# Stores of the high parts of parked weights: issued from GpSimd, one operation later, in place of ScalarE

## The chip, the core and the metric

The kernel runs on one core of one Trainium2 chip. The metric is the device time of one execution in microseconds, from the first to the last instruction of the core.

## What is computed

Causal attention over 4 batches, 8 heads, 576 positions and 64 features (four heads with a local window of 32 positions, four with a stride of 32), and behind it two gated feed-forward blocks over 2304 tokens, with 512 features and 1536 hidden ones. Cut to what matters:

```
scores = q @ k.T / 8, masked; attn = softmax(scores); x = attn @ v      # x: 2304 x 512
xn = x / sqrt(mean(x*x) + 1e-6) * rms_g
x  = (silu(xn @ w1_gate) * (xn @ w1_val)) @ w1_out
out = (silu(x @ w2_gate) * (x @ w2_val)) @ w2_out
```

All tensors are float32. The kernel forms each float32 product with fp32r matmuls: it splits each operand into a high and a low part and sums three products, high x high, high x low and low x high.

## The kernel before, in words

**Tiling and stages.** Three stages overlap. Attention (the class Attention, in program order up to about 260 us of the trace) makes x in pieces. The first four chunks of the first block's hidden features run beside it and a little after it, in plain products of 128 x 512 tokens (`gate`, `down`). From then on a *block stage* runs over five passes of four chunks and three stretches of 768 tokens each (the loop over `work` at the end). There each pair of projections, gate and value, is done with seven products of quarter size in place of eight: sums and differences of quarters of the weights and of the tokens go in. A chunk's weights are therefore sums of quarters (`QUARTERS`), split into high and low.

**The weights' way.** A `combined_step(m, c, how)` prepares gate and value weights of chunk c. Its operations are: load the two raw blocks (`fetch`, SP's queue), decode them with ScalarE and VectorE (`scale`, lines 279 to 296), form four sums of quarters on GpSimd (`sum_`, line 385), and split the four groups into high and low. `first` (line 424) casts the high part on ScalarE, `second` (line 431) subtracts it on VectorE for the low part. With how = "park" the parts go to DRAM instead of staying in SBUF: both parts lie in the step's own raw and dh buffers, `first` sends the high part off ScalarE's queue, and `save` (line 438) sends the low part off SP's. A later `recall_step` loads both back (`w<-pk`), 512 KB or 256 KB at a time. The buffers raw (three) and dh (two) are reused by the next step once both stores have landed. There are sixteen steps with how = "park" (the words with p in `plan`): p14 to p17 first, twelve in the block stage.

**The order.** The operations of a step run in the order of this list, one at a time, between the matmuls of other work:

```
ops = [op(i, f) for i, f in ((0, first), (0, second), (1, first), (0, save), (1, second), (2, first), (1, save), (2, second),
                             (3, first), (2, save), (3, second), (3, save))]
```

`point()` is called every few matmuls; it advances attention's phases and, through `weights()`, starts operations at the rate `pace["op"]` (0.7 to 1.0 per point in the block stage). `behind(eng)` puts an instruction after the engine's last important one in program order; `paced` makes a GpSimd instruction wait for a given matmul. Within these rules the framework orders each engine's queue, and every engine runs its queue in order.

**GpSimd's other work** is the normalisation of attention's exponentials (`e`, line 700), sums of token quarters (lines 1169 and 1339), the weights' sums (line 385), and in the block stage the low halves of the next stretch's tokens:

```
with behind("act"):
    nc.scalar.copy(out=xh[:, kk], in_=src[:, kk])
paced(nc.gpsimd.tensor_tensor(out=xl[:, kk], in0=src[:, kk], in1=xh[:, kk].bitcast(F32), op=ALU.subtract), ("pe", None))
```

(lines 1357 and 1358.) GpSimd issues two transfers of its own, loads of k for the first batch (line 554).

**ScalarE's other work** near the change: attention's exponentials (line 683), copies out of PSUM (line 87: pT, qT, kT, x), the casts of tokens (line 981), and in the block stage the copies and activations of lines 1415 to 1439.

Of the kernel before, what the change touches and what calls it, by code (L numbers as in the profile page):

```python
# [8 lines left out]
F32 = mybir.dt.float32  # L9
# [16 lines left out]
def attn_ffn_ffn(ctx: ExitStack, tc: tile.TileContext, q, k, v, w1g, w1v, w1o, rms_g, w2g, w2v, w2o, out):  # L26
    nc = tc.nc
# [19 lines left out]
    dp = ctx.enter_context(tc.tile_pool(name="dp", bufs=1, space=DRAM))  # L47
# [92 lines left out]
    def paced(ins, by="act"):  # L140
        if by in last:
            tc.add_manual_dep(ins_of(ins), (last[by][2] if by == ("pe", None) else last[by]).name, mybir.DependencyInfo(mybir.DependencyClass.Sync, mybir.DependencyReason.DATA),
                              reason="pace")
# [10 lines left out]
    def send(out, in_):  # L154
        n = 4
        for w in out.shape:
            n *= w
        line[0] = max(line[0], clock[0]) + n / state['rate']
        nc.sync.dma_start(out=out, in_=in_)
# [61 lines left out]
    def take(key, kb):  # L221
        place = room[kb].pop(0)
        held.setdefault(key, []).append((kb, place))
        return place
# [5 lines left out]
    def home(place, w, name):  # L230
        pool, tag = place
        return pool.tile([128, 2, w], F32R, tag=tag, name=name)
# [6 lines left out]
    def back(bk, n):  # L239
        bk["back"].append((clock[0] + (6 if n else 0) + state["slack"], n))  # L240
# [7 lines left out]
    def spent(bk, n):  # L248
        bk["wback"].append(clock[0] + n)
        bk["wback"].sort()  # L250

    def spaces():
        bk = racks[0]
        while bk["back"] and bk["back"][0][0] <= clock[0]:
            bk["free"] += bk["back"].pop(0)[1]
        return bk["free"]
# [3 lines left out]
    def fetch(m, c, z, cell):  # L260
        bk = cell["bk"] = racks[0]
        bk["free"] -= 1
        w = WSRC[m][z].bitcast(U32)
        if z == 2:
            src = w[c * 128:(c + 1) * 128, :].rearrange("p (k f) -> p k f", k=KC)
        else:
            src = w[:, c * 256:(c + 1) * 256].rearrange("(k p) f -> p k f", p=128)
        r = bk["pool"].tile([128, KC, 256], U32, tag="raw", name="raw", bufs=bk["bufs"])
        send(out=r, in_=src)
        words = r.rearrange("p k f -> p (k f)").rearrange("p (n s) -> p n s", s=2)  # L270
        cell.update({"raw": r, "lw": words[:, :, 0], "hw": words[:, :, 1]})
# [84 lines left out]
    def combined_step(m, c, how):  # L356

        g, v = {}, {}
        at = []
        parts = []  # L360
        got = {}
        n4 = 2 if how == "split" else 3

        def ready():
            if spaces() < 2:
                return False
            return how == "park" or len(room[4]) >= n4 and len(room[2]) >= 7 - 2 * n4

        def load():
            if how != "park":  # L370
                at.extend([take((m, c, False), 4) for _ in range(n4)] + [take((m, c, False), 2) for _ in range(7 - 2 * n4)])
            fetch(m, c, 0, g)
            fetch(m, c, 1, v)

        def source(z):
            flat = g["raw"].rearrange("p k f -> p (k f)").bitcast(F32)
            t = flat.rearrange("p (a n) -> p a n", a=4)
            b11, b21 = g["h"][:, 0:256], g["h"][:, 256:512]
            b12, b22 = v["h"][:, 0:256], v["h"][:, 256:512]
            return flat, t, b22, {0: (b12, b11), 2: (b22, b12), 1: (b22, t[:, 0]), 3: (b21, t[:, 1])}[z]  # L380

        def sum_(z):
            def f():
                _, t, _, (a, b) = source(z)
                paced(nc.gpsimd.tensor_tensor(out=t[:, z], in0=a, in1=b, op=ALU.subtract))  # L385
            return f

        def sums():
            sum_(3)()
            flat, _, b22, _ = source(0)  # L390
            spaces = v["raw"].rearrange("p k f -> p (k f)").bitcast(F32)
            src = {0: g["h"], 1: flat[:, 0:512], 2: flat[:, 512:1024], 3: b22}
            his = {0: spaces[:, 0:512], 1: spaces[:, 512:1024], 2: spaces[:, 0:512], 3: v["h"][:, 0:256]}
            for i in (0, 3, 1, 2) if how != "park" else (0, 1, 3, 2):
                w = 256 * len(QUARTERS[i])
                if how == "park":
                    parts.append((QUARTERS[i], src[i], his[i].bitcast(F32R), src[i].bitcast(F32R), i))
                    continue
                if how == "split" and i == 1:
                    places = [(q_, src[i][:, 256 * j:256 * j + 256], at[n4 + 1 + j]) for j, q_ in enumerate(QUARTERS[i])]  # L400
                    places = [((q_,), a, p) for q_, a, p in places]
                else:
                    places = [(QUARTERS[i], src[i], at[n4] if i == 3 else at[min(i, n4 - 1)])]
                for qs, a, place in places:
                    t_ = home(place, 256 * len(qs), f"w{m}_{c}_{qs[0]}")
                    parts.append((qs, a, t_[:, 0], t_[:, 1], t_))

        stores = {}

        def op(i, f):  # L410
            def g_():
                f(*parts[i])
                if f is (save if how == "park" else second) and parts[i][0][0] in (1, 3):
                    spent((g if parts[i][0][0] == 1 else v)["bk"], 6 if how == "park" else 8)
                if i == len(parts) - 1 and f is (save if how == "park" else second):
                    back(g["bk"], 1)
                    if how == "park":
                        back(v["bk"], 1)
                    else:
                        wt[m, c, 0] = got  # L420
                        wdone.add((m, c, 0))
            return g_

        def first(qs, a, hi_, lo_, t_):
            with behind("act"):
                nc.scalar.copy(out=hi_, in_=a)
                if how == "park":
                    stores[t_] = d = dp.tile([128, 2, 256 * len(qs)], F32, name=f"pk{m}_{c}_{t_}")
                    nc.scalar.dma_start(out=d[:, 0], in_=hi_.bitcast(F32))

        def second(qs, a, hi_, lo_, t_):
            with behind("dve"):
                nc.vector.tensor_tensor(out=lo_, in0=a, in1=hi_.bitcast(F32), op=ALU.subtract)
            if how != "park":
                for j, q_ in enumerate(qs):
                    got[q_] = t_[:, :, 256 * j:256 * j + 256]

        def save(qs, a, hi_, lo_, t_):
            d = stores[t_]
            send(out=d[:, 1], in_=lo_.bitcast(F32))  # L440
            parked.setdefault((m, c), {})[t_] = d

        k = 5 if how == "split" else 4
        lag = 1 if how == "park" else 2
        if how == "park":
            ops = [op(i, f) for i, f in ((0, first), (0, second), (1, first), (0, save), (1, second), (2, first), (1, save), (2, second),
                                         (3, first), (2, save), (3, second), (3, save))]
            ops[2].late = 1
        else:
            ops = [op(i, f) for i in range(k) for f in (first, second)]  # L450
            ops[lag * 2].late = 1
        sv = scale(v, int(how != "park"))
        sv[0].late = 0.6
        return Step([load] + scale(g, 0) + sv + [sum_(0), sum_(2), sum_(1), sums] + ops, ready, PRIO_W)
# [26 lines left out]
    def behind(eng):  # L481

        return tc.issue_after(last[eng]) if eng in last else nullcontext()
# [1064 lines left out]
    for n, (m, cs, t0) in enumerate(work):  # L1548
# [88 lines left out]
        c = chunks[-1]  # L1637
# [47 lines left out]
```

## Time and profile before

| | |
|---|---|
| median of 3 runs | 1016.6 us (1012.5 to 1017.88) |
| the profiled execution's own time, and its span | 1012.5 us |
| TensorE busy | 967.9 us, 5987 matmuls |
| VectorE, ScalarE, GpSimd busy | 579.2, 576.7, 387.0 us |
| transfers on ScalarE's queue (q10) | 14.68 MB, 4.0% of the time of 16 DMA engines |
| transfers on SP's queue (q1) | 203.72 MB, 61.8% |
| transfers on GpSimd's queue (q0) | 0.28 MB, 0.1% |

The profile is of one execution. Busy time counts instructions that compute; the issue of a transfer is not counted on ScalarE and SP (rows marked ACTq and SPq in the timelines). In the rows, ACT is ScalarE, DVE VectorE, POOL GpSimd, PE TensorE, SP the engine that issues most transfers. `out<-in` are the program's names of tiles; pk is the store in DRAM, raw and dh the step's buffers, w a weight tile, xh and xl a token tile's high and low part. PEclk is the granted clock of TensorE as a share of full speed. An entry in brackets is idle time of the engine just before the instruction, and what ended it.

### The profile page before, as it was taken

Reading aid. Unit: us, or ns where it says so; the run is one execution under the profiler, and the core shown is the slowest. Engines: PE = TensorE matmul, PEld = TensorE weight load, DVE = VectorE, ACT = ScalarE, POOL = GpSimd, SP = SyncE. Lnnn points to the kernel's source line nnn. Section 1 sums busy time; section 2 is a strip of 40 time slices with the busy share of each in tenths; the row PEclk is TensorE's granted clock in tenths of the full one; section 3 lists DMA queues with packets and bytes.
Section 4 is the critical chain, followed back from the end, with each engine's and each line's share of the span. In section 5 each row is a group of like instructions: output and inputs, shape, how many; then the busy total and the mean of one; then the engine's idle time right before and its main releaser. Section 6 shows DMA issues by size and latency. Waiting matters only on the chain.

```text
span 1012.5 us, 17613 instructions
## 1 busy us (share of the span) xinstructions
PE 967.9 (96%) x5987; PEld 889.2 (88%) x5987; DVE 579.2 (57%) x1294; ACT 576.7 (57%) x1449; POOL 387.0 (38%) x417
## 2 busy tenths in 40 slices
PE   5789998799999999999999999999999999999998
PEld 4677876577989999998999999999999999999997
DVE  2886575777434665465655566554556655653333
ACT  5988586674344645464655555555646655563431
POOL 3221052352050546270716464663517243441500
PEclk9988999899999999999999999999999999999999
DMA  7775647955978374988667777637887397865211
GB/s 185 208 227 184 171 127 218 290 187 184 341 236 295 118 242 153 319 285 287 193 204 264 261 223 252 200 132 281 271 299 269 123 309 249 307 203 174 83 65 63
DMA packets 171602, 219.81 MB, mean 217 GB/s; under 512 B 47092, under 2 KB 125116, under 8 KB 171512
## 3 DMA queue, kind: packets, MB, share of 16 engines
q1 hardware_dynamic: 162104, 203.72, 61.8%
q10 hardware_dynamic: 9216, 14.68, 4.0%
q8 instruction: 47, 0.77, 0.3%
q14 instruction: 43, 0.35, 0.1%
q0 software_dynamic: 192, 0.28, 0.1%
HBM read 146.80 MB, written 71.83 MB: 216 GB/s over the span
## 4 chain that ended last, share of the span: by engine, by line
PE 70%; DMA 3%; ACT 2%; DVE 1%; issue 0%; SPq 0%; DVEq 0%; ACTq 0%
PE b_y L76 32%; PE b_a L76 17%; PE b_g L76 11%; PE b_v L76 10%; DMA pk<-raw 1%; DMA pk<-dh 1%; DMA raw<-in_moe_w_gate_dram 0%; DMA xq<-xst 0%; ACT xh L1357 0%; ACT dh L279 0%; ACT hh L1439 0%; ACT t L1415 0%; ACT raw L287 0%; DVE dh L296 0%; ACT t L1429 0%
## 5 line engine op out<-in xcount | busy, mean ns | idle before, releaser
L1358 POOL TENSOR_TENSOR xl<-xst,xh 128x384 fp32r<-128x384 f32 x196 | 212.2, 1105 | 177.4 <-PE b_y L76 78.0
L76 PE MATMUL b_y<-xh,w 128*128 128x384 f32 x784 | 211.4, 335 | 2.6 <-ACT t L1415 2.2
L76 PEld LDWEIGHTS b_y<-xh,w 128*128 128x128 f32 x784 | 142.9, 188 | 5.7 <-ACT t L1415 3.1
L76 PE MATMUL b_a<-xh,w 128*128 128x384 f32 (+2 forms) x512 | 141.0, 335 | 0.8 <-ACT t L1415 0.7
L76 PE MATMUL b_y<-xl,w 128*128 128x384 f32 x392 | 131.4, 335 | 0.0
L76 PE MATMUL b_g<-xh,w 128*128 128x384 f32 (+2 forms) x416 | 127.6, 348 | 2.2 <-ACT w L304 1.5
L76 PE MATMUL b_v<-xh,w 128*128 128x384 f32 (+2 forms) x352 | 108.1, 350 | 2.0 <-ACT t L1429 1.3
L76 PEld LDWEIGHTS b_a<-xh,w 128*128 128x128 f32 x512 | 93.2, 188 | 4.1 <-ACT t L1415 1.8
L1357 ACT CAST xh<-xst 128x384 fp32r<-128x384 f32 x196 | 91.5, 520 | 0.0
L385 POOL TENSOR_TENSOR raw<-dh 128x256 f32<-128x256 f32 x40 | 29.4, 754 | 150.9 <-DVE dh L296 56.3
L76 PE MATMUL b_a<-xl,w 128*128 128x384 f32 (+2 forms) x256 | 85.8, 335 | 0.0
L76 PEld LDWEIGHTS b_g<-xh,w 128*128 128x128 f32 x416 | 77.4, 191 | 7.9 <-ACT w L304 1.7
L76 PE MATMUL b_y<-hh,w 128*128 128x384 f32 (+2 forms) x304 | 80.7, 341 | 0.0
L76 PEld LDWEIGHTS b_y<-xl,w 128*128 128x128 f32 x392 | 73.6, 188 | 1.8
L700 POOL TENSOR_TENSOR e<-e,rc 128x384 f32<-128x384 f32 (+3 forms) x40 | 36.3, 915 | 98.4 <-DVE nb L674 23.4
L76 PEld LDWEIGHTS b_v<-xh,w 128*128 128x128 f32 x352 | 64.9, 190 | 7.9 <-ACT t L1429 1.7
L76 PE MATMUL b_g<-xl,w 128*128 128x384 f32 (+2 forms) x208 | 70.3, 338 | 0.0
L76 PE MATMUL b_y<-w,hh 128*128 128x512 f32 x216 | 67.1, 391 | 0.0
L683 ACT ACTIVATE e<-e,nb 128x96 f32<-128x96 f32 (+2 forms) x152 | 56.6, 376 | 13.6 <-DVE nb L674 9.6
L76 PE MATMUL b_v<-xl,w 128*128 128x384 f32 (+2 forms) x176 | 59.5, 338 | 0.0
L76 PEld LDWEIGHTS b_y<-hh,w 128*128 128x128 f32 x304 | 54.7, 188 | 2.7
L1435 DVE TENSOR_TENSOR b_y<-b_y,t 128x384 f32<-128x384 f32 x56 | 31.6, 565 | 43.1 <-ACT b_y L1429 42.2
(206 smaller groups left out, 2141.0 us busy)
## 6 DMA issues: line engine op xcount, KB each, us to landing
w<-pk SPq DMA_DIRECT2D x48, 512.0 KB
raw<-in_moe_w_gate_dram SPq DMA_DIRECT2D x24, 512.0 KB
raw<-in_moe_w_val_dram SPq DMA_DIRECT2D x24, 512.0 KB
raw<-in_moe_w_out_dram SPq DMA_DIRECT2D x24, 512.0 KB
pk<-raw ACTq DMA_DIRECT2D x48, 256.0 KB
part<-ob SPq DMA_DIRECT2D x48, 256.0 KB
xst<-y_d SPq DMA_DIRECT2D x30, 384.0 KB
xst<-xq SPq DMA_DIRECT2D x28, 384.0 KB
```

Source lines behind the costliest of these rows:

```text
L76: traced(nc.tensor.matmul(out_, a, b_, start=start, stop=stop, **how))
L385: paced(nc.gpsimd.tensor_tensor(out=t[:, z], in0=a, in1=b, op=ALU.subtract))
L683: r = nc.scalar.activation(out=e[:qn, i, :kn], in_=e[:qn, i, :kn], func=AF.Exp, bias=nb[:qn, i:i + 1], scale=-1.0, accum_out=sums[:qn, i:i ...
L700: eng.tensor_tensor(out=e[:qn, :nt, :kn], in0=e[:qn, :nt, :kn], in1=rc[:qn, :nt].unsqueeze(2).to_broadcast([qn, nt, kn]), op=ALU.mult)
L1357: nc.scalar.copy(out=xh[:, kk], in_=src[:, kk])
L1358: paced(nc.gpsimd.tensor_tensor(out=xl[:, kk], in0=src[:, kk], in1=xh[:, kk].bitcast(F32), op=ALU.subtract), ("pe", None))
L1435: nc.vector.tensor_tensor(out=s, in0=s, in1=v, op=ALU.mult)
```

## The change

The store of the high part goes from `first`, behind the cast on ScalarE's queue, to the head of `second`, onto GpSimd's queue. Neither the cast nor the subtraction changes, nor the number of bytes; the destination in DRAM is created in `second`.

```diff
--- before.py
+++ after.py
@@ -424,11 +424,11 @@
         def first(qs, a, hi_, lo_, t_):
             with behind("act"):
                 nc.scalar.copy(out=hi_, in_=a)
-                if how == "park":
-                    stores[t_] = d = dp.tile([128, 2, 256 * len(qs)], F32, name=f"pk{m}_{c}_{t_}")
-                    nc.scalar.dma_start(out=d[:, 0], in_=hi_.bitcast(F32))
 
         def second(qs, a, hi_, lo_, t_):
+            if how == "park":
+                stores[t_] = d = dp.tile([128, 2, 256 * len(qs)], F32, name=f"pk{m}_{c}_{t_}")
+                nc.gpsimd.dma_start(out=d[:, 0], in_=hi_.bitcast(F32))
             with behind("dve"):
                 nc.vector.tensor_tensor(out=lo_, in0=a, in1=hi_.bitcast(F32), op=ALU.subtract)
             if how != "park":
```

In the order above `(0, second)` comes one entry after `(0, first)`; the other three come two entries after theirs, with a `save` or a `first` of another group between.

## Rows read from the trace of the kernel before

**Rows 1.** Part 1 of the page: busy us (share of the span) xinstructions
```profile
PE 967.9 (96%) x5987; PEld 889.2 (88%) x5987; DVE 579.2 (57%) x1294; ACT 576.7 (57%) x1449; POOL 387.0 (38%) x417
```

**Rows 2.** The table by stretches: busy us of each engine, PEclk, DMA share, GB/s
```profile
175.00:200.00 25.00, 18.73 (x115) 14.43 (x114) 18.43 (x74) 15.71 (x57) 9.76 (x12) 0.86 0.94 282
260.00:1012.50 752.50, 743.85 (x4040) 706.09 (x4038) 403.35 (x664) 391.73 (x845) 305.90 (x306) 1.00 0.66 222
```

**Rows 3.** The list of TensorE's waits: us in total, times, longest
```profile
PE b_y L76 <- ACT t L1415: 2.2, 1, 2.2
...
PE b_v L76 <- ACT t L1429: 1.3, 1, 1.3
```

**Rows 4.** The view of tile pk: durations in ns (min/median/max), first and last start
```profile
L429 ACTq DMA_DIRECT2D pk<-raw x48: 326/326/387, 144.2 to 884.4; - x48
...
L159 SPq DMA_DIRECT2D pk<-raw x32: 319/322/962, 164.2 to 890.3; - x32
L429 ACTq DMA_DIRECT2D pk<-dh x16: 326/352/1028, 150.6 to 882.5; - x16
```

**Rows 5.** Timeline of ScalarE, 176 to 200 us: start, us, ..., [idle before <-releaser]
```profile
178.97 0.51 ACT L87 COPY qT<-b_a 64x432 f32<-64x432 f32 x1 [1.55 <-PE b_y L76]
...
181.83 0.19 ACT L683 ACTIVATION_READ_ACCUMULATOR e<-e,nb 126x1 f32 x1
185.56 0.33 ACTq L429 DMA_DIRECT2D pk<-dh  x1
185.94 0.40 ACT L683 ACTIVATE e<-e,nb 126x126 f32<-126x126 f32 x1 [3.92 <-DMA xst<-x_d]
...
195.72 0.60 ACT L981 CAST xh<-xraw 128x512 fp32r<-128x512 f32 x1
```

**Rows 6.** Timeline of ScalarE, 147 to 157 us
```profile
148.66 0.65 ACT L426 CAST raw<-raw 128x512 fp32r<-128x512 f32 x1
150.58 0.33 ACTq L429 DMA_DIRECT2D pk<-dh  x1
150.95 0.58 ACT L87 COPY pT<-b_a 96x512 f32<-96x512 f32 x1 [1.64 <-PE b_y L76]
```

**Rows 7.** Timeline of TensorE, from 146 to 204 us
```profile
147.44 0.64 PE L80 MATMUL b_a<-ident,e 128*96 128x128 f32 x4
...
156.94 0.69 PE L76 MATMUL b_y<-pT,vl 96*64 96x64 f32 x16 [2.14 <-ACT pT L87]
...
179.53 0.37 PE L76 MATMUL b_a<-kT,qT 64*126 64x126 f32 x1 [0.38 <-ACT qT L87]
...
191.45 1.10 PE L80 MATMUL b_a<-ident,e 126*126 126x126 f32 x4 [5.59 <-POOL e L700]
...
201.16 0.48 PE L76 MATMUL b_g<-xh,w 128*128 128x512 f32 x1
```

**Rows 8.** Timeline of VectorE, 178 to 198 us
```profile
186.85 0.17 DVE L693 TENSOR_SCALAR sums<-sums 126x4 f32<-126x4 f32 x1 [2.34 <-ACT e L683]
```

**Rows 9.** Timeline of GpSimd, from 176 to 412 us
```profile
179.77 0.77 POOL L385 TENSOR_TENSOR raw<-dh,raw 128x256 f32<-128x256 f32 x1
190.37 1.03 POOL L700 TENSOR_TENSOR e<-e,rc 126x504 f32<-126x504 f32 x1 [9.83 <-DVE sums L693]
...
402.28 8.93 POOL L1358 TENSOR_TENSOR xl<-xst,xh 128x384 fp32r<-128x384 f32 x8
```

**Rows 10.** The table by stretches, in four stretches of one microsecond
```profile
157.00:158.00 1.00, 1.00 (x18) 0.88 (x19) 0.00 (x0) 1.00 (x4) 0.51 (x1) 1.00 0.87 302
195.00:196.00 1.00, 1.00 (x4) 0.70 (x4) 0.14 (x2) 1.00 (x6) 0.00 (x0) 0.50 1.08 377
196.00:197.00 1.00, 1.00 (x6) 0.91 (x5) 0.64 (x2) 1.00 (x4) 0.03 (x1) 0.56 1.09 374
477.00:478.00 1.00, 0.50 (x3) 0.50 (x4) 0.90 (x2) 0.45 (x2) 0.00 (x0) 1.00 1.07 424
```

**Rows 11.** Groups of GpSimd by line: busy us, mean ns | idle before
```profile
L554 POOL DMA_DIRECT2D kn<-in_k_dram x2 | 1.4, 718 | 0.5 <-issue 0.5
```

## The prediction

> **What bounds the kernel now.** I read the page's busy table first: TensorE is busy for 967.9 us of a span of 1012.5 us, and no other engine for more than 579.2 us [rows 1]. A gain can only come out of the 44.6 us in which TensorE stands, or out of stretches in which its clock is low. The table by stretches says where those are: from 260 us to the end TensorE works for 743.85 of 752.50 us, while between 175 and 200 us it works for 18.73 of 25 and its granted clock is 0.86 of full speed [rows 2]. The list of TensorE's waits names what is left after 260 us: 2.2 and 1.3 us behind ScalarE's copies of product banks [rows 3]. So I look for the moved transfers between 140 and 260 us, where the attention stage still runs. Four of the sixteen steps that store weights (planned as p14 to p17; four stores of high parts each) lie there.
>
> The view of the tile pk shows the 64 issues on ScalarE's queue, 48 of raw and 16 of dh, 326 ns in the middle [rows 4]. That is 48 x 0.326 + 16 x 0.352 = 21.3 us of ScalarE, which is busy for 57% [rows 1]. The timelines show more than the issue time. At 185.56 ScalarE issues the store of a dh whose cast was done before; it had been idle since 182.02 (181.83 + 0.19), for 3.92 us, and the profile names as releaser the landing of SP's load xst<-x_d, which the store doesn't read [rows 5]. The same happens twice more, smaller: after the cast at 148.66 ScalarE stands for 1.64 us until the issue at 150.58, although the transposes that its next copy reads were done at 147.44 + 0.64 = 148.08; and the qT copy at 178.97 comes after 1.55 us of standing [rows 5 to 7]. What stands in ScalarE's queue behind such an issue is attention work.
>
> **The change part by part.** It removes 64 issues and their waits from ScalarE, adds 64 to GpSimd's queue, and starts each store one operation of the planner later.
>
> *First stand (150.58).* TensorE later idles 2.14 us at 156.94 for a pT copy [rows 7]. The 1.64 us come off that idle time: -1.6 us. Ends: 0 and -2.1.
>
> *Second stand (178.6).* TensorE idles 0.38 us at 179.53 for the qT copy behind it [rows 7]: -0.4 us.
>
> *Third stand (185.56).* The two exponentials of the first group that come after 185.94 could start 3.9 us earlier. VectorE takes over: its sums at 186.85 came after 2.34 us of standing, so that is what its own queue can move up [rows 8]. GpSimd's normalisation follows at 190.37 after 9.83 us of idleness, and TensorE's transposes end an idle time of 5.59 us at 191.45 [rows 7, 9]. So -2.3 us (ends 0 and -3.9), and about 3.2 us of the idle time stay.
>
> *The clock.* After those 5.59 us the granted clock reads 0.50 (1.2 GHz); the 0.56 of the stretch from 196 to 197 us puts its return to full (2.4 GHz) at about 196.9. After the idle times of 2.14 and 2.2 us it reads 1.00 [rows 10]. TensorE works from 191.45 to 196.9 at half rate and loses 2.7 us. An idle time of 3.2 us is nearer to 2.2 than to 5.6, so I take the fall as gone: -2.7 us. Ends: 0 and -2.7.
>
> Together -1.6 - 0.4 - 2.3 - 2.7 = -7.0 us.
>
> *What is given back.* TensorE would reach the next segment's first product (201.16) 7.0 us earlier. Its high halves begin with a cast at 195.72 to 196.32 out of a load [rows 5, 7]: a cover of 4.8 us. If the load stays where it is, 2.2 us come back; if SP's loads move up as well, none (SP's queue is given nothing by the change, and nothing is taken from it). The DMA engines are 94% busy in that stretch [rows 2], which speaks for the first; fewer stores in the way speak for the second. I take the middle, +1.1.
>
> *GpSimd's issues.* The trace has two, loads of 108 rows, 718 ns each [rows 11]. A store has 128 rows: 718 x 128 / 108 = 0.85 us, an estimate by rows (0.72 by count, 1.36 by bytes, 256 against 135 KB). 64 x 0.85 = 54 us take GpSimd from 387 to 441 us, under half of the span. In the block stage 12 x 4 = 48 of them fall on an engine busy for 305.90 of 752.50 us, 41% [rows 2]: some 20 meet work and push back what is queued behind, the low halves xl of the next block (up to eight in a row, 8.93 us [rows 9]). TensorE is who waits for those. Without cover that is 20 x 0.85 = +17 us; with cover 0. TensorE's list of waits names no xl at all [rows 3], so I take +0.5, about half of one store in the longest run.
>
> *GpSimd's wait.* Each store now waits on GpSimd for ScalarE's cast. One operation later that cast is over; behind the wait stand the normalisations of e and the low halves, and TensorE waits for both. GpSimd is idle from 180.5 (179.77 + 0.77) to 190.37 [rows 9], so I take 0; what a longer wait costs stands with the second rival.
>
> *The later start.* The last high part leaves ScalarE at 884.4, the low part of the same step leaves SP at 890.3 [rows 4]. The buffer, and the load that recalls the weights, wait for both; a start one operation later stays inside those 5.9 us: 0. If that cover were gone, the next raw load would be late by the rest.
>
> *ScalarE after 260 us.* Its issues cost nothing now, since TensorE waits for ScalarE 3.5 us there [rows 3], behind copies and not behind an issue: 0, at most -3.5.
>
> Sum: -7.0 + 1.1 + 0.5 = -5.4 us. Against the profiled execution's own 1012.5 us that is 1007.1. That execution is the fastest of the three runs; the median is 1016.6, 4.1 us above, and with the same difference comes to **1011.2**.
>
> *A rule that speaks against it.* The rows say that a store's issue held ScalarE for up to 3.92 us [rows 5]. The Trainium skill, page "DMA: Bandwidth & Descriptors", section "Issuing engines are not separate DMA queues", says that transfers from all engines run on the same DMA engines, and that issuing from several saves only the issuing time. By that rule of the Trainium skill the stands would come back elsewhere and the time would be 1016.6 us; the trace doesn't agree as far as ScalarE goes, which lost far more than its issuing time.
>
> **The rivals.**
>
> *Freed, but not kept (no change).* The loads of the stretch at 94% set its end: the second and third stand turn into waits for loads, the clock falls as before, and only the first 1.6 us stay: 1015.0. For it: a store moved is still the same bytes. Against: what TensorE waits for at 191.45 is arithmetic, not a load. This is what the rule of the Trainium skill above would make of the change.
>
> *The change doesn't take the wait away.* GpSimd's queue may wait for foreign landings as ScalarE's did, 3.92 us at most. At 181 to 186 that is harmless, GpSimd being idle until 190.37 [rows 9]; later it is not. With two GpSimd transfers in the whole trace nothing excludes it. The gain of 5.4 us is then spent on halves that come late: between 1011 and 1020, middle 1015.5.
>
> *GpSimd's queue becomes the bound (slower).* Its place is the block stage, its price the 20 stores that meet work, 20 x 0.85 = 17 us, and it decides from the point at which the cover of the low halves is shorter than the stores put in front of them: 1016.6 - 7.0 + 1.1 + 17 = 1027.7. For it: the casts of a whole step can fall into one run of halves, as GpSimd's row at 402.28 is eight of them without a break [rows 9]. Against: no wait of TensorE for them now [rows 3]. The Trainium skill, page "SBUF — State Buffer", section "SBUF: two separate sides", describes how VectorE can shut GpSimd out so that it can't write a transfer's descriptors, with some 3.1 us for a transfer that takes 0.62 alone. By that figure of the Trainium skill 20 x 3.1 = 62 us would be added without cover, an estimate; no run here shows it.
>
> **How the numbers follow.** A measurement of this kernel can tell about 0.5%, 5.1 us (its three runs lie 5.4 us apart): faster means under 1011.5, slower over 1021.7. Forecast 0.52; its own range is 1006 to 1014, and I give 0.44 to the part under 1011.5, since the fall of the clock and the first stand can each add some, and 0.08 to the part above. Freed but not kept 0.28, not taken away 0.08, GpSimd as the bound 0.12. So faster 0.44, same 0.08 + 0.28 + 0.08 = 0.44, slower 0.12. The range reaches down to 1004 (1016.6 less the 7.0 us, the 3.5 us after 260 us, and 2.1 for the runs' spread) and up to 1020, over the two rivals without a change; it leaves out the slower rival and a small rest below.
>
> **What would show it.** Right: no issue on ScalarE's queue at line 429; no stand of ScalarE near 150, 178 and 182 to 186; the idle time before the transposes of e near 187 under 4 us and the clock at 1.00 after it; 64 more transfers on GpSimd of 0.7 to 1.4 us; no xl among TensorE's waits. Wrong: an idle time of 5 us or more and a clock of 0.50 between 185 and 200 us, waits for qn, kn or xraw in its place, or low halves that TensorE waits for after 260 us.

## The result and the profile after

The changed kernel takes 1020.1 us (median of 7 runs, 1018.5 to 1022.8) against 1014.5 us for the kernel before on the same chip (7 runs): ratio 1.0054, 95% interval 1.0032 to 1.0076. It is **slower by 0.54%, some 5.5 us**, where 5.4 us less were forecast.

The profiled execution has a span of 1020.7 us (its own time is 1022.5, 2.4 us above the median). Busy times, and three stretches of the changed kernel (busy us of each engine, PEclk, DMA share, GB/s), against [rows 1, 2]:

```profile
PE 972.4 (95%) x5987; PEld 891.5 (87%) x5987; DVE 594.2 (58%) x1294; ACT 576.0 (56%) x1449; POOL 418.2 (41%) x481
```

```profile
175.00:200.00 25.00, 16.81 (x93) 12.73 (x91) 19.45 (x71) 13.78 (x53) 10.45 (x15) 0.80 0.93 272
...
260.00:1020.70 760.70, 749.77 (x4047) 709.95 (x4047) 416.85 (x669) 392.09 (x847) 328.64 (x354) 1.00 0.66 221
675.00:700.00 25.00, 21.93 (x97) 19.24 (x96) 13.56 (x13) 10.66 (x23) 14.64 (x17) 0.86 0.65 229
```

GpSimd has its 64 transfers more and is busy for 31 us more; VectorE, which the change doesn't touch, is busy for 15 us more. The stretch from 175 to 200 us, where most of the forecast gain lay, lost: TensorE works there for 16.81 us in place of 18.73, with the clock at 0.80 in place of 0.86. And a stretch of the block stage that was full before is now broken, 675 to 700 us.

TensorE's timeline, changed kernel (start, us, ..., the idle time ahead of it and its releaser):

```profile
123.53 0.43 PE L76 MATMUL b_a<-kT,qT 64*108 64x108 f32 x2 [0.46 <-DVE x L882]
...
154.80 0.69 PE L76 MATMUL b_y<-pT,vl 96*64 96x64 f32 x16 [0.93 <-ACT pT L87]
...
180.37 0.34 PE L76 MATMUL b_y<-kT,qT 64*108 64x108 f32 x1 [1.73 <-DVE nb L674]
...
192.67 1.10 PE L80 MATMUL b_a<-ident,e 126*126 126x126 f32 x4 [6.46 <-POOL e L700]
...
251.83 0.50 PE L76 MATMUL b_v<-xh,w 128*128 128x512 f32 x1 [1.21 <-DVE sg L965]
...
686.86 0.69 PE L76 MATMUL b_g<-xh,w 128*128 128x384 f32 x1 [3.07 <-DVE ob L89]
...
771.16 0.41 PE L76 MATMUL b_y<-xh,w 128*128 128x384 f32 x1 [0.98 <-DMA w<-pk]
```

Two of these products serve as posts, since TensorE's order from the first of them on is the same in all kernels here but for names. In the kernel before they stand at:

```profile
124.78 0.43 PE L76 MATMUL b_a<-kT,qT 64*108 64x108 f32 x2 [0.47 <-DVE x L882]
...
250.21 0.50 PE L76 MATMUL b_v<-xh,w 128*128 128x512 f32 x1 [0.68 <-DVE sg L965]
```

From the first post to the second took 125.43 us and takes 128.30 (+2.9, the attention stage); from the second to the span's end 762.29 and 768.87 (+6.6, the block stage). The start before the first post is 1.25 us shorter; no store stands there, and over the twelve traces it lies between 121.5 and 124.9 us. So two places have to be explained.

**Attention stage.** The first stand went nearly as forecast: the idle time before the product of pT is 0.93 in place of 2.14 us [rows 7]. The idle time before the transposes of e grew, 6.46 in place of 5.59. ScalarE's timeline shows why (changed kernel; compare [rows 5]):

```profile
177.28 0.40 ACT L426 CAST dh<-dh 128x256 fp32r<-128x256 f32 x1
183.52 1.14 ACT L981 CAST xh<-xraw 128x512 fp32r<-128x512 f32 x2 [5.84 <-DMA xraw<-x_d]
184.57 0.62 ACT L426 CAST raw<-raw 128x512 fp32r<-128x512 f32 x1
185.09 0.40 ACT L683 ACTIVATE e<-e,nb 126x126 f32<-126x126 f32 x1
...
190.12 0.60 ACT L426 CAST raw<-raw 128x512 fp32r<-128x512 f32 x1
```

Two token casts of line 981, which stood at 195.72 behind the exponentials, now stand ahead of them and wait 5.84 us for their load. (SP's order changed too: that load is issued at 179.15, where the kernel before issues its first load of xraw in this stretch at 189.06.) The first exponential starts at 185.09; in the kernel before it is this row:

```profile
181.14 0.40 ACT L683 ACTIVATE e<-e,nb 126x126 f32<-126x126 f32 x1
```

One wait was taken off ScalarE's queue, and a longer one moved into its place.

**Block stage.** VectorE's, GpSimd's and SP's timelines of the changed kernel at 679 us:

```profile
679.17 7.03 DVE L433 TENSOR_TENSOR raw<-raw 128x512 fp32r<-128x512 f32 x1
686.12 0.68 DVE L89 COPY ob<-b_g 128x512 f32<-128x512 f32 x1
```

```profile
679.24 0.56 POOL L431 DMA_DIRECT2D pk<-raw  x1
679.82 5.83 POOL L1358 TENSOR_TENSOR xl<-xst,xh 128x384 fp32r<-128x384 f32 x6
```

```profile
676.81 0.32 SPq L159 DMA_DIRECT2D xq<-xst  x1
686.23 0.32 SPq L159 DMA_DIRECT2D pk<-raw  x1
```

and of the kernel before at the same instructions:

```profile
678.67 1.55 DVE L433 TENSOR_TENSOR raw<-raw 128x512 fp32r<-128x512 f32 x1
680.34 0.69 DVE L89 COPY ob<-b_g 128x512 f32<-128x512 f32 x1
```

```profile
678.66 6.34 POOL L1358 TENSOR_TENSOR xl<-xst,xh 128x384 fp32r<-128x384 f32 x6 [1.13 <-ACT xh L1357]
```

Before, the subtract met the start of a run of six halves on GpSimd and lasted 1.55 us: one half (about 1 us) and its own time. Now a GpSimd store stands ahead of the run, and the subtract ends half a microsecond behind the whole run. The copy that empties TensorE's bank b_g stands behind it on VectorE, so TensorE idles 3.07 us; SP's next store waits for the subtract too, and SP issues nothing for 9 us. The stretch from 675 to 700 us has a granted clock of 0.86 (in it 0.50, 1.2 GHz, behind that idle time).

Only two of the 64 GpSimd stores stand directly ahead of an unbroken run of five halves or more. The other one, at 440.33, shows the same hold, shorter because VectorE comes to it in the middle of the run (VectorE, then GpSimd, changed kernel):

```profile
443.27 3.10 DVE L433 TENSOR_TENSOR raw<-raw 128x512 fp32r<-128x512 f32 x1 [0.38 <-ACT raw L426]
```

```profile
440.91 4.90 POOL L1358 TENSOR_TENSOR xl<-xst,xh 128x384 fp32r<-128x384 f32 x5
```

In the kernel before this subtract takes 0.95 us. TensorE pays little for this hold: a wait of 0.6 us for VectorE's hl.

### The profile page after: what moved, and what is told of

It reads as the page before. It is cut to its first block, busy times and chain, and to the rows that moved or that the text cites. A ratio compares the mean times of both kernels' runs of the same rounds, so it can differ in the third digit from the quotient of the medians.

```text
span 1020.7 us, 17673 instructions
## 1 busy us (share of the span) xinstructions
PE 972.4 (95%) x5987; PEld 891.5 (87%) x5987; DVE 594.2 (58%) x1294; ACT 576.0 (56%) x1449; POOL 418.2 (41%) x481
## 4 chain that ended last, share of the span: by engine, by line
PE 68%; DMA 4%; DVE 2%; ACT 2%; issue 1%; POOL 0%; ACTq 0%; DVEq 0%; SPq 0%; POOLq 0%
PE b_y L76 32%; PE b_a L76 15%; PE b_g L76 11%; PE b_v L76 9%; DMA w<-pk 2%; DMA pk<-dh 1%; DMA pk<-raw 1%; DMA raw<-in_moe_w_out_dram 0%; ACT xh L1357 0%; DVE dh L296 0%; ACT dh L279 0%; ACT hh L1439 0%; POOL raw L385 0%; DVE dh L433 0%; DVE raw L433 0%
## 5 line engine op out<-in xcount | busy, mean ns | idle before, releaser
L1358 POOL TENSOR_TENSOR xl<-xst,xh 128x384 fp32r<-128x384 f32 x196 | 209.2, 1088 | 132.3 <-PE b_y L76 56.7
```

## The experiments

Two theories, then: **V**, VectorE held beside GpSimd's store and run; **Q**, the order of ScalarE's queue. The rivals are L, the later start of the stores, and chance. The table gives each kernel's ratio to the kernel before (with its interval), TensorE's idle time before the transposes of e, and the time between the posts and behind the second one in its profile, less that of the kernel before. The two stretches are of one execution each: between 124 and 250 us programs with the same stores there differ by 1 to 2 us, and the 35 runs of the kernel before that belong to the first four experiments lie between 1010.7 and 1021.6 us. The ratios therefore say how much, and the stretches only where.

| kernel | ratio (95%) | idle before e, us | 124 to 250, us | 250 to end, us |
|---|---|---|---|---|
| changed | 1.0054 (1.0032 to 1.0076) | 6.46 | +2.9 | +6.6 |
| queue_only | 1.0033 (1.0015 to 1.0050) | 6.58 | +2.6 | +4.0 |
| place_only | 0.9995 (0.9972 to 1.0018) | 2.72 | +1.2 | -0.7 |
| early_moved | 1.0011 (0.9993 to 1.0028) | 7.56 | +4.5 | -0.9 |
| late_moved | 1.0007 (0.9984 to 1.0030) | 3.41 | -1.2 | +3.8 |
| one_store | 1.0051 (1.0026 to 1.0076) | 5.36 | +2.8 | +3.8 |
| casts_behind | 0.9993 (0.9969 to 1.0016) | 0.32 | -1.7 | +5.0 |
| casts_early | 0.9995 (0.9974 to 1.0017) | 0.54 | -1.7 | +8.0 |
| one_store2 | 1.0006 (0.9986 to 1.0027) | 4.58 | +3.5 | -0.1 |
| casts_one | **0.9960** (0.9940 to 0.9979) | 1.65 | -2.6 | -0.3 |
| casts_sp | 1.0040 (1.0021 to 1.0060) | 0.32 | -1.8 | +8.2 |

### The change taken apart

**queue_only**: GpSimd issues, as early as before.

```diff
         def first(qs, a, hi_, lo_, t_):
...
-                    nc.scalar.dma_start(out=d[:, 0], in_=hi_.bitcast(F32))
+                    nc.gpsimd.dma_start(out=d[:, 0], in_=hi_.bitcast(F32))
```

Expected: 

> Only the queue is changed: the store of the high part is issued by GpSimd in `first`, behind the cast, as early as before. Theory V (VectorE's two-input subtract is held while GpSimd issues a store and then runs its low halves without a break): the same 64 stores stand on GpSimd, so holds of some us should appear somewhere among VectorE's subtracts and the time should be 0 to 6 us above before, the size set by where they fall. Theory L (the later start makes the recalls and the buffers late): nothing is late, so the time should be as before or up to 3 us under it. Theory Q (ScalarE's queue takes another order, token casts that wait for their load stand ahead of the exponentials): 1 to 3 us above before, if the order comes out as in the changed kernel, with an idle time of about 6 us ahead of the transposes of e near 190 us.

**place_only**: ScalarE issues, at the head of `second`.

```diff
         def second(qs, a, hi_, lo_, t_):
...
-                nc.gpsimd.dma_start(out=d[:, 0], in_=hi_.bitcast(F32))
+                nc.scalar.dma_start(out=d[:, 0], in_=hi_.bitcast(F32))
```

Expected: 

> Only the place is changed: ScalarE still issues the store, at the head of `second`. Theory V: GpSimd issues none, so no subtract of VectorE lasts over 2 us after 260 us, and the block stage loses nothing; within 2 us of before. Theory L: the loss of 5.6 us stays whole, and the load of a recalled weight at about 771 us is again what TensorE waits for. Theory Q: the stands of ScalarE behind its store stay as before the change, near 150, 178 and 185 us; the time is within 2 us of before unless the casts move.

The queue alone costs 0.33%, and its trace has both faults: the casts wait 6.18 us at 181.46, and the subtract lasts 7.03 us at 677.22. The place alone costs nothing that shows (0.9972 to 1.0018), and in its trace TensorE waits for no recalled weight behind 260 us. **L falls** as the cause, as the prediction had it.

**early_moved** and **late_moved**: the change in the steps p14 to p17 alone, and in the other twelve alone.

```diff
-                nc.gpsimd.dma_start(out=d[:, 0], in_=hi_.bitcast(F32))
+                if (m, c) in ((1, 4), (1, 5), (1, 6), (1, 7)):
+                    nc.gpsimd.dma_start(out=d[:, 0], in_=hi_.bitcast(F32))
```

(early_moved; the others keep the store of before in `first`. late_moved has `not in`.)

Expected: 

> The change alone in the four steps of the attention stage (p14 to p17); the twelve others store as before. Theory V: the hold at 679 us is gone, so most of the 5.6 us: 0 to 2 us above before. Theory Q: what the attention stage lost stays: the idle time ahead of the transposes of e near 190 us is about 6 us, the clock falls to 0.50 behind it, and the time is 2 to 3 us above before. Theory L: as V.

Expected: 

> The reverse: the change in the twelve steps of the block stage alone, the four early ones store as before. Theory V: one or more subtracts of VectorE of over 2.5 us after 260 us beside GpSimd's low halves, and 3 to 6 us above before. Theory Q: the attention stage is as before, and so is the time, within 2 us. Theory L: 1 to 3 us above before, with a recall that TensorE waits for.

The table splits by stage: early_moved loses in the attention stage alone (+4.5, -0.9), late_moved in the block stage alone (-1.2, +3.8), with the same subtract:

```profile
672.78 7.04 DVE L436 TENSOR_TENSOR raw<-raw 128x512 fp32r<-128x512 f32 x1
```

(L436 is line 433 of the others, moved by three lines.) By the medians each half loses less than expected, and neither interval excludes no change; which half weighs more can't be read from these two runs.

Over all the kernels: the casts wait ahead of the exponentials in every one whose early steps store from GpSimd (unless they are put back, below), and in neither of those whose early steps store from ScalarE. Why the framework moves them was not tried.

### Theory Q by itself

**casts_behind**: the changed kernel, with the casts of this one segment put behind the last exponentials issued so far.

```diff
             def exp():
...
+                last["exp"] = ins_of(r)
...
-            ra = nc.scalar.copy(out=xh[:, :n], in_=xc)
+            with behind("exp" if si == 3 else "none"): ra = nc.scalar.copy(out=xh[:, :n], in_=xc)
```

Expected: 

> The changed kernel, with the four token casts of the segment that begins at about 200 us put behind the exponentials on ScalarE. Theory Q (these casts, waiting 5.84 us for their load ahead of the exponentials, ate the third stand): the exponentials start near 179 to 181 us, TensorE's idle time before the transposes of e falls from 6.46 to about 3 us or less, the clock holds, and 3 to 5 us come back: 1 to 3 us above before. Rival (the loads or VectorE set the end of that stretch anyway): the idle time stays at 5 us or more, or moves into a wait for xh or w, and the time stays 5 us above before.

```profile
179.39 0.62 ACT L426 CAST raw<-raw 128x512 fp32r<-128x512 f32 x1 [0.68 <-POOL raw L385]
...
181.19 0.40 ACT L683 ACTIVATE e<-e,nb 126x126 f32<-126x126 f32 x1 [1.18 <-DVE nb L674]
...
193.42 2.16 ACT L981 CAST xh<-xraw 128x512 fp32r<-128x512 f32 x4
```

```profile
175.00:200.00 25.00, 22.17 (x143) 16.44 (x142) 20.56 (x76) 16.86 (x60) 12.49 (x17) 0.86 0.92 284
```

(ScalarE's timeline and the stretch from 175 to 200 us of casts_behind.) The casts wait for nothing at 193.42, the exponentials run through, and TensorE's idle time before the transposes of e falls from 6.46 to 0.32 us. TensorE works for 22.17 us of the stretch. 1.0054 falls to 0.9993, some 6 us, with the two intervals leaving 3 us either way, although the hold at 675 us is still there (7.00 us in this trace). Q is shown; of the price, the 3 to 5 us expected are not excluded.

The 0.32 us is not all gain, and the clock did not hold as expected. TensorE's timeline of casts_behind, and one microsecond of it:

```profile
181.42 0.34 PE L76 MATMUL b_y<-kT,qT 64*108 64x108 f32 x1 [1.75 <-DVE nb L674]
...
189.10 0.65 PE L80 MATMUL b_a<-ident,e 126*126 126x126 f32 x4 [0.32 <-POOL e L700]
```

```profile
184.00:185.00 1.00, 1.00 (x5) 0.81 (x3) 1.00 (x3) 1.00 (x6) 0.00 (x0) 0.50 1.21 289
```

Behind a wait of 1.75 us for VectorE's nb the clock reads 0.50 from 182 to 188 us, so the work ahead of the transposes is stretched and fills time that would else be idle. By the first post (124.83 here) the transposes begin after 64.27 us, against 69.14 in the changed kernel and 66.67 in the kernel before: 4.9 and 2.4 us earlier. The wait for nb stands in all nine kernels whose early steps store from GpSimd (1.58 to 1.75 us; 0.31 before, 0.92 in place_only and late_moved). What makes it was not tried.

### Theory V by itself

**one_store** was to take the store at 679.24 us off GpSimd, and named the wrong step: the one it moved stands near 606 us.

```diff
-                nc.gpsimd.dma_start(out=d[:, 0], in_=hi_.bitcast(F32))
+                (nc.scalar if (m, c, t_) == (2, 3, 2) else nc.gpsimd).dma_start(out=d[:, 0], in_=hi_.bitcast(F32))
```

Expected: 

> The changed kernel, but of its 64 stores one, group 2 of the step for chunk 3 of the second block (the one issued at 679.24 us beside the subtract of 7.03 us), goes off ScalarE at the same place. Theory V (this transfer ahead of six halves without a break holds VectorE): the subtract falls to 0.7 to 1.6 us, TensorE's idle time of 3.07 us and the low clock behind it are gone, and 5 to 6 us come back: within 1 us of before. Rival (any store there is late, whoever issues it; or the loss is spread over all GpSimd stores): 4 us or more above before.

With 1.0051 it repeats the changed kernel: one store more or less elsewhere changes nothing, and the hold (7.00 us at 677.69) stays. It says nothing on V.

**one_store2** moves the right one.

```diff
-                nc.gpsimd.dma_start(out=d[:, 0], in_=hi_.bitcast(F32))
+                (nc.scalar if (m, c, t_) == (2, 5, 2) else nc.gpsimd).dma_start(out=d[:, 0], in_=hi_.bitcast(F32))
```

Expected: 

> The run one_store moved the store issued at 606 us and left the one beside the subtract of 7 us where it was. Here the store at 679.24 us itself (group 2 of the step for chunk 5 of the second block) goes off ScalarE, all else as in the changed kernel. Theory V: the subtract falls to 1.6 us or less, TensorE's idle time of 3.07 us and the low clock behind it are gone; 4 to 6 us less than the changed kernel, so 0 to 2 us above before. Rival (the casts on ScalarE are nearly the whole loss, what is lost at 686 us is caught up behind it): within 2 us of the changed kernel, 4 us or more above before.

```profile
680.34 1.54 DVE L433 TENSOR_TENSOR raw<-raw 128x512 fp32r<-128x512 f32 x1
681.99 0.69 DVE L89 COPY ob<-b_g 128x512 f32<-128x512 f32 x1
```

```profile
675.00:700.00 25.00, 25.00 (x129) 22.86 (x128) 12.27 (x20) 14.07 (x30) 15.53 (x17) 1.00 0.88 327
```

One of 64 stores off GpSimd, and the subtract lasts 1.54 us, TensorE works for all 25 us of the stretch at full clock, and the ratio falls from 1.0054 to 1.0006, 4.9 us, with the intervals leaving 3 us either way. V is shown for this place. In the table, the five kernels with this hold lose 3.8 to 6.6 us behind 250 us, and the four without it and with no other over 3 us (place_only, early_moved, one_store2, casts_one) gain 0.1 to 0.9. The shorter hold near 440 us stays in one_store2 and casts_one (2.62 and 2.69 us).

**hold_alone** and **hold_alone2** take the same instructions out of the kernel.

```diff
+            if c == "d":
+                r = nc.gpsimd.dma_start(out=d, in_=hi.bitcast(F32))
+            else:
+                r = nc.gpsimd.tensor_tensor(out=xls[i], in0=w[:, 1, :384], in1=hi[:, :384].bitcast(F32), op=ALU.subtract)
...
+        put("dve", nc.vector.tensor_tensor(out=lo, in0=w[:, 2], in1=hi.bitcast(F32), op=ALU.subtract), gate)
```

(hold_alone2, where the gate is a chain of copies on ScalarE whose length is stepped; in hold_alone all halves go into one tile, and VectorE has two subtracts.)

Expected: 

> Nothing of the reference is computed: GpSimd's run of 128x384 subtracts (6 or 12) and two 128x512 subtracts of VectorE alone on the chip, with and without a GpSimd store of 128x512 ahead of the run, VectorE starting with it or some 2.5 us into it. Theory V: without the store VectorE's first subtract takes at most 1.0 + 0.7 us (one GpSimd instruction and its own), behind a store it takes as long as the run has left: some 6 us with six, some 12 with twelve, 3 to 4 when it starts in the middle. Rival (the hold needs something else of the full kernel, traffic of the DMA engines or waits between the halves): at most 2 us everywhere.

Expected: 

> Nothing of the reference is computed. GpSimd's run of eight halves again, now each into a tile of its own so that they follow without a gap, once plain and once with a store as the second instruction; one subtract of VectorE begins in ten steps of some 40 ns later and later into the run. Theory V: the plain run holds it for one instruction (up to 1.7 us) at every step, the one with the store until the run's end (5 us or more). Rival (the hold is a matter of the instant at which the subtract meets the run, not of the store): both kinds hold it at some steps and not at others. Second rival (it needs the traffic of the full kernel): at most 2 us everywhere.

In hold_alone no single subtract takes over 1.82 us, behind a store or not: V missed there. But its halves start 1.07 us apart and last 0.99, so each is followed by a pause of 0.08 us, while in the kernel each starts 0.03 to 0.06 us before the one before it has ended. hold_alone2 removes the pause (0.95 us apart). VectorE and GpSimd in its first three sections, plain, behind a store, plain:

```profile
9.00 1.26 DVE L66 TENSOR_TENSOR lo<-w,hi 128x512 fp32r<-128x512 f32 x1 [9.00 <-ACT a L58]
17.82 6.69 DVE L66 TENSOR_TENSOR lo<-w,hi 128x512 fp32r<-128x512 f32 x1 [7.56 <-ACT a L58]
27.52 1.23 DVE L66 TENSOR_TENSOR lo<-w,hi 128x512 fp32r<-128x512 f32 x1 [3.00 <-ACT a L58]
```

```profile
6.82 8.09 POOL L64 TENSOR_TENSOR xl<-w,hi 128x384 fp32r<-128x384 f32 x8 [6.37 <-ACT a L52]
...
16.57 0.69 POOL L62 DMA_DIRECT2D d<-hi  x1
17.28 6.68 POOL L64 TENSOR_TENSOR xl<-w,hi 128x384 fp32r<-128x384 f32 x7
25.30 8.10 POOL L64 TENSOR_TENSOR xl<-w,hi 128x384 fp32r<-128x384 f32 x8 [1.34 <-ACT a L52]
```

All ten plain sections give 0.91 to 1.26 us, all ten behind a store 6.2 to 6.7 us: to the end of the run, 17.28 + 6.68 = 23.96, and the subtract's own time. The instant, stepped over some 0.35 us, doesn't matter. So the store ahead of an unbroken run is enough, without the kernel's traffic.

It is not the only way in. In **casts_early** (GpSimd stores in the four early steps, ScalarE in `second` in the others, casts behind) VectorE is held at 398.70 us by eight halves with no store ahead of them (GpSimd's and VectorE's timelines):

```diff
-                nc.gpsimd.dma_start(out=d[:, 0], in_=hi_.bitcast(F32))
+                (nc.gpsimd if (m, c) < (1, 8) else nc.scalar).dma_start(out=d[:, 0], in_=hi_.bitcast(F32))
```

Expected: 

> GpSimd stores in the four early steps alone, ScalarE stores (one operation later) in the other twelve, and the casts stand behind the exponentials: both suspected losses are out. Theories V and Q together: no subtract of VectorE over 2 us after 260 us, the idle time near 190 us at about 3 us or less, the first stand gone as in the changed kernel: 2 to 6 us under before. Rival (what the attention stage gains is taken back by loads at the segment's start): as before, within 1.5 us.

```profile
398.64 7.78 POOL L1358 TENSOR_TENSOR xl<-xst,xh 128x384 fp32r<-128x384 f32 x8
```

```profile
398.70 8.27 DVE L433 TENSOR_TENSOR dh<-dh,raw 128x512 fp32r<-128x512 f32 x1 [0.93 <-POOL raw L385]
```

This subtract takes 1.5 us in ten of the twelve traces of the kernel, 8.27 here and 3.43 in one_store. One trace of each can't tell how often it comes. It costs here as well: by the second post the stores behind it are issued some 6 us later than in the kernel before, ScalarE's decoding of the next step waits for their landing, and TensorE for ScalarE:

```profile
428.41 0.66 ACT L279 ACTIVATE dh<-raw 128x512 f32<-128x512 f32 x1 [6.96 <-DMA pk<-dh]
```

```profile
429.50 0.69 PE L76 MATMUL b_v<-xh,w 128*128 128x384 f32 x1 [6.08 <-ACT t L1429]
```

That, with the clock at 0.50 behind it (428 to 434 us), is where this kernel's profile loses its 8.0 us in the block stage. Its ratio, 0.9995, is no better than casts_behind's.

### A version that beats both

**casts_one** has both mends in the changed kernel, casts_behind and one_store2.

```diff
-                nc.gpsimd.dma_start(out=d[:, 0], in_=hi_.bitcast(F32))
+                (nc.scalar if (m, c, t_) == (2, 5, 2) else nc.gpsimd).dma_start(out=d[:, 0], in_=hi_.bitcast(F32))
...
-            ra = nc.scalar.copy(out=xh[:, :n], in_=xc)
+            with behind("exp" if si == 3 else "none"): ra = nc.scalar.copy(out=xh[:, :n], in_=xc)
```

Expected: 

> Both mends in the changed kernel: the token casts behind the exponentials, and the one store at 679 us off ScalarE. If both losses are real and add, 3 to 6 us under before, and 3 to 6 under casts_behind. Rival (the second is caught up, or comes back as a wait for a recalled weight near 766 us): within 2 us of before.

```profile
175.00:200.00 25.00, 20.45 (x143) 15.10 (x140) 21.56 (x78) 17.25 (x61) 14.18 (x17) 0.93 0.92 289
675.00:700.00 25.00, 25.00 (x136) 23.64 (x135) 11.21 (x20) 13.05 (x28) 10.38 (x12) 1.00 0.77 287
```

1010.9 us against 1014.9: 0.9960 (0.9940 to 0.9979), faster than the kernel before by 4.0 us and the only one here with an interval below 1. The two prices add roughly: 6.2 us (casts) and 4.9 us (store) from the changed kernel would make -5.6 us against before, and -4.0 were measured. Between casts_behind and casts_one the store is worth 3.3 us.

**casts_sp** gives the twelve late steps to SP in place of GpSimd, with the casts behind as above.

```diff
-                nc.gpsimd.dma_start(out=d[:, 0], in_=hi_.bitcast(F32))
+                (nc.gpsimd if (m, c) < (1, 8) else nc.sync).dma_start(out=d[:, 0], in_=hi_.bitcast(F32))
```

Expected: 

> GpSimd stores in the four early steps, SP in the other twelve, the casts behind the exponentials. No GpSimd store stands near its runs of halves in the block stage, and ScalarE issues none either. Theory V: no subtract over 2 us after 260 us beside a store, no idle time of 3 us near 686: 2 to 6 us under before. Rival (VectorE's subtracts are held by runs of halves whether a store stands ahead of them or not, as the 8.27 us at 398.7 us of casts_early hint): one or more subtracts over 2.5 us again, and within 2 us of before.

No subtract is held over 1.6 us, as V says, and yet it is slower by 0.40%: in its trace TensorE waits 1.95 us at 448 us for a low half hl and 2.67 us at 766.53 for a recalled weight. Which of the waits in SP's queue does it was not followed up; SP is not a free place for these stores.

## Why the prediction was wrong

**The steps that failed.** *Third stand* (-2.3) and *the clock* (-2.7): they took ScalarE's queue as it stood in the trace of before, less one store. The framework gave it another order, and casts waiting 5.84 us for their load took the store's place. Both terms went to the other side: 6.46 us of idle time, and the clock at 0.50 behind it. With the order put back, casts_behind reaches the transposes 2.4 us earlier than the kernel before, 1.2 of them by the first stand, so that, net of the second stand, about half of the third stand's -2.3 can be seen as won. The rival "freed, but not kept" had the right form, a wait for a load, but not the right place: no load sets the end of that stretch, a cast put ahead of its need does.

*The clock* failed by its own argument as well: it took the fall as gone because 3.2 us of idle time are nearer to 2.2 than to 5.6. In the changed kernel the clock falls to 0.50 (1.2 GHz) behind the 1.73 us at 180.37 already (181 to 184 us), and behind 3.07 us at 686.86; in one_store it stays at 1.00 behind 3.0 us at the same place. The length of the idle time alone did not decide, and no kernel here won this term whole.

*Second stand* (-0.4): the 0.38 us are gone, but the wait for VectorE's nb behind it grew from 0.31 to 1.73 us, with that first fall of the clock behind it. VectorE's part in that stretch was in no term.

*GpSimd's issues* (+0.5): the price and its bearer were wrong. A store costs 0.56 us, not 0.85 (below). No TensorE wait names an xl, as forecast; what pays is VectorE, which no term had. One store of 64 costs some 5 us, by the place at which it stands. The rival "GpSimd's queue becomes the bound" had sign and stage right, but counted 20 stores that push halves back, when one that holds VectorE decides. Its 17 us were three times the loss.

*GpSimd's wait* (0): it took ScalarE's cast as over one operation later. 22 of the 64 stores wait for it, 57.8 us in total, and at one point TensorE pays. In the changed kernel VectorE's reciprocal for the first group of e is there at 190.01, but ahead of the normalisation stands the store at 191.02, waiting for ScalarE's cast of 190.12, which ends at 190.72. (The profile names the sg of VectorE, which ended last before it; another store starts 0.3 us behind its cast as well, at 185.48.) That is some 1.5 us of the 6.46 (VectorE, then GpSimd):

```profile
189.84 0.17 DVE L694 RECIPROCAL rc<-sums 126x4 f32<-126x4 f32 x1
```

```profile
191.02 0.54 POOL L431 DMA_DIRECT2D pk<-raw  x1 [4.98 <-DVE sg L958]
191.57 2.87 POOL L700 TENSOR_TENSOR e<-e,rc 126x504 f32<-126x504 f32 x3
```

*The base.* The profiled execution was taken for the fastest run by setting its span beside the runs' times. A run's time lies some 1.8 us above its span (1022.5 and 1020.7 for the changed kernel), so it took about 1014.3 us, and over seven runs the kernel before has a median of 1014.5: the base of 1016.6 was 2.1 us too high. This moved the forecast up, toward what was measured.

*Readings.* The 3.92 and 1.64 us of standing are ScalarE's idle times up to its next computation and hold the issue's own 0.33; to the issue they are 3.54 and 1.27 us. And *What is given back* (+1.1) took SP's queue as untouched, while its order changed; with nothing won ahead of it, no run shows the term.

**The steps that held.** *First stand*: -1.2 us of the -1.6 (2.14 to 0.93); with ScalarE issuing, place_only keeps idle times of 1.06 and 2.60 us there. *Later start*: 0, by place_only; the 0.98 us for a recalled weight at 771.16, which neither queue_only nor place_only has, is not explained. *ScalarE after 260 us*: taken as 0, with -3.5 as its end. The waits of 1.3 and 2.2 us [rows 3] are gone from TensorE's list, but early_moved, where ScalarE's late stores stay as they were, shows at most 0.4 us for either, so that the change took them away isn't shown; one_store2 and casts_one, which have no late stores on ScalarE but one, gain 0.1 and 0.3 us in the block stage.

*Not taken away* did not come: no landing of another transfer is among what GpSimd's stores wait for. The instructions in the traces show where ScalarE's foreign waits came from, and it is the program: before its store at 185.56 ScalarE waits for semaphore 111 (a counter that engines wait on), the one that the store's own landing raises, and the transfer that used it last is SP's xst<-x_d of 179.76. SP's 793 transfers and ScalarE's 64 share eight such semaphores; GpSimd's transfers have eight of their own.

What the prediction asked to look for gave the verdict: no issue at line 429, but an idle time over 5 us and a clock of 0.50 between 185 and 200 us, a wait for xraw in its place.

## What to carry to other kernels

Where the framework orders the queues, a transfer moved off one engine changes what stands in that engine's queue: before a stand is booked as won, ask which waiting instruction can move into its place, and after the change read the order of the queue that was freed, not only the one that was loaded. A transfer on GpSimd ahead of an unbroken run of GpSimd arithmetic is priced by the length of that run wherever VectorE then has a two-input instruction on SBUF to do (shown here for float32 subtracts), so look for the one place where TensorE stands behind it rather than multiply a count by a mean. And two small losses can hide one gain: the version with both mended is faster than either kernel.

## What the runs showed of the hardware

- **A GpSimd store holds VectorE through the run behind it.** Alone, VectorE's subtract of two SBUF tiles takes 0.9 to 1.3 us beside a plain run of GpSimd, and 6.2 to 6.7 us when a store stands ahead of seven halves that follow without a pause. With pauses of 0.08 us it takes at most 1.82. The Trainium skill, page "SBUF — State Buffer", section "SBUF: two separate sides", says that a VectorE instruction with two SBUF inputs and a GpSimd instruction that reads SBUF shut each other out, the first to start holding for its whole instruction. The plain runs agree with it (one half of about 1 us is waited for at most); behind a store the measurement differs, since the hold lasts for the whole run.
- The same hold came without a store in two traces of twelve (8.27 and 3.43 us at one subtract). What starts it there is open.
- **GpSimd's issue of a store** takes 0.54 to 0.66 us, nearly the same for 128 and for 256 KB; the two loads of before, of 135 KB, took 0.72. The view of the tile pk, changed kernel (durations in ns, min/median/max):

```profile
L431 POOL DMA_DIRECT2D pk<-raw x48: 539/557/660, 145.5 to 892.6; - x48
...
L431 POOL DMA_DIRECT2D pk<-dh x16: 539/539/604, 148.6 to 890.9; - x16
```
